# Window attention and two feed-forward layers on one core: a key ring of three blocks, a value block loaded twice, and earlier weight loads

## The chip, the cores and the metric

The kernel runs on 1 core of a Trainium2 chip. The metric is the device time of one execution in microseconds (us). It stands at 888.23 us before, the median of 3 runs (887.37 to 889.02).

## What is computed

Windowed attention (4 batches, 8 heads, 576 positions, head size 64, a window of 64 positions), and behind it two dense layers with 2304 tokens, d_model 512 and d_ff 2048. The weights are float64 in memory and are split on the chip into a high and a low float32r part; q, k and v are float32.

```python
scores = scale * np.matmul(q, k.transpose(0, 1, 3, 2))
rel = pos[:, None] - pos[None, :]
mask = (rel >= 0) & (rel < window)
attn = softmax(where(mask, scores, -1e9))
x = matmul(attn, v)                      # to (2304, 512)
r = np.maximum(x @ w_in, 0.0);  x = (r * r) @ w_out          # first layer
h = x @ w_in2;  out = (np.maximum(h, 0.0) + np.log1p(np.exp(-np.abs(h)))) @ w_out2
```

## The kernel before, in words

The 2304 rows are 18 "pairs" p of two 64-row blocks (a pair is 128 rows of all 8 heads). One pair runs through these jobs, whose names the text uses:

- Lq, Lk, Lv: loads of 256 KB each, issued by SyncE (SP). A row of a head is 64 floats.
- TK, TQ: transposes on TensorE (PE, line 528). CK, CQ: their copies out of PSUM, by VectorE (DVE) or ScalarE (ACT); CK writes `kT`, CQ scales q.
- CW (line 532, DVE): moves the last key block of the pair before to the third block of `kT`, since a pair needs its own two key blocks and the one before. V (line 611, DVE): copies the first 64 value rows of pair p into the buffer of pair p-1, so that one buffer holds the two value blocks that go together.
- S: mask and score matmuls on PE (lines 549 and 556); M (line 572, DVE): row maximum; E (line 581, ACT): exponent; N (lines 590 to 593, DVE): normalisation; PT, CP: transpose of the probabilities and copy; PV (line 619, PE): times the values; XH (ACT, line 630) and XL (DVE, line 633): x split into two parts.

The first layer runs over token tiles 0 to 4 of 384, 384, 512, 512 and 512 rows; pairs 0 to 2 make tile 0, pairs 3 to 5 tile 1. For tiles 0 and 1 a chunk f (128 of the 2048 hidden columns) of tile t is L0_t_f (x times w_in: 12 matmuls, lines 709 to 712), then Re, Sq and the split Gh (ACT) and Gl (DVE, line 757), then K0_t_f (times w_out: 12 matmuls, line 736). Each chunk needs a piece of w_in (f, 0) and of w_out (f, 1). A piece is loaded (LW, 512 KB, lines 350 and 355), then A (ACT, line 374), B, C, D, E (DVE, lines 377 to 393), F (ACT, line 400), G (DVE, line 404): five DVE steps each. Pieces then go to memory and are read back for the later tiles and the second layer, which work in blocks of seven products (PA to PD, lines 908 to 911). RZ (line 445) and SS (line 457) are DVE work on pieces for those blocks.

The order of all of it is worked out at build time by `Plan.order`, a list scheduler with a cost for each job and due times made from the table `WANTED`; every engine then runs its list in order, so an instruction that waits holds all behind it on its engine. At the start PE first waits for q of pair 0, transposes it, and runs 8 matmuls on an identity (`warm`, line 1097) that do nothing but run; they wait in the plan for `begin`, the clearing of `kT` and of a buffer of zero values (lines 1089 to 1091).

Of the kernel before, what the change touches and what calls it, by code (L numbers as in the profile page):

```python
# [10 lines left out]
F32 = mybir.dt.float32  # L11
# [11 lines left out]
    R0=254.26, RS=-0.27, T0=91.05, STEP0=0.29, A1=56.67, STEP1=4.99, B0=68.41, STEPB=2.68,  # L23
    T1=106.21, T2=160.86, LAP=93.92, C0=174.36, C1=484.25, PAIRS=106.74, SPAN=32.29,
# [155 lines left out]
def window_attention_moe_moe2(  # L180
# [80 lines left out]
    masks = const.tile([P, 3, P], BF16, name="masks")  # L261
    kT = const.tile([P, HP, P + W], F32, name="kT")
# [3 lines left out]
    def sel(m, a, half, pattern, base, mult):  # L266
        s = masks[W * a:W * a + W, m, W * half:W * half + W]
        nc.gpsimd.affine_select(
            out=s, in_=s, pattern=[[pattern, W]], compare_op=ALU.is_ge,
            fill=MASKED, base=base, channel_multiplier=mult,  # L270
        )

    def make_masks():


        nc.gpsimd.memset(masks, 0.0)
        for m in range(3):
            for a in range(2):
                own, before = (0, 1) if a == 0 else (1, 0)
                sel(m, a, own, -1, 0, 1)  # L280
                if m == a + 1:
                    sel(m, a, before, 0, -1, 0)
                else:
                    sel(m, a, before, 1, -1, -1)
# [72 lines left out]
    def add_weights(ph, n, f, which, want):  # L357
# [48 lines left out]
        def store(j):  # L406
# [12 lines left out]
            take=[("c", None, 1, [raw])] if ph else [], lag=3.2 if ph else 2.2,  # L419
            close=[("pro", (f"w1_{f}", 512 * i)) for i in range(2)] if not ph and late else [],  # L420
# [74 lines left out]
    def add_pair(p, at, step, loads_after):  # L495
# [7 lines left out]
        mask = masks[:, (1 if p in FIRST else 2 if p in FIRST2 else 0), :].rearrange("p (o f) -> p o f", o=1)  # L503
        mask = mask.to_broadcast([P, HP, P])
# [5 lines left out]
        def load(src, name):  # L510
            def fn(j):
                t = place(j, name, [P, DM], F32).rearrange("p (h d) -> p h d", h=H)
                done = 0
                while done < P:
                    b, s = divmod(p * P + done, S)
                    n = min(P - done, S - s)
                    nc.sync.dma_start(  # L517
                        out=t[done:done + n], in_=src[b, :, s:s + n, :].rearrange("h p d -> p h d")
                    )
                    done += n  # L520
            return fn
# [22 lines left out]
        def score(j):  # L544
            sc = [place(j, f"sc{p}_{e}", [P, HP, P], F32) for e in range(2)]
            qt = heads(live[f"q{p}"])
            if early:
                for e in range(2):
                    nc.tensor.matmul(out=sc[e], lhsT=ident16, rhs=mask, start=True, stop=False)

            for c in range(HP):
                kc = kT[:, c, :].rearrange("p (w s) -> p w s", w=3)
                for a in range(2):
                    for e in range(2):
# [4 lines left out]
                            rhs=kc[r, 0:2, :] if a else kc[r, 0:3:2, :],  # L559
# [3 lines left out]
        def add_mask(e):  # L563
            def fn(j):
                nc.vector.tensor_tensor(out=pr(e), in0=live[f"sc{p}_{e}"], in1=mask, op=ALU.add)
            return fn
# [76 lines left out]
        before = (f"S{p - 1}",) if p else ()  # L643
        for src, name in ((k, f"k{p}"), (q, f"q{p}"), (v, f"v{p}")):
            add(f"L{name}", {"DMA": 1.1}, load(src, name), loads_after, take=piece(name), lag=2.4, choice=from_top)
# [652 lines left out]
```

## Time and profile before

| what | value |
|---|---|
| median of 3 runs | 888.23 us |
| the profiled execution, its own time | 887.61 us |
| its span, first to last instruction | 885.8 us |
| granted TensorE clock, mean | 0.996 |
| PE busy | 859.0 us (97%) |
| DVE busy | 740.3 us (84%) |
| ACT busy | 596.1 us (67%) |
| moved by DMA | 254.35 MB, 287 GB/s |

The span is the time between first and last instruction of the profiled execution; 1.8 us of its own time lie around it. "Busy" counts overlapping instructions of one engine once; an engine that is busy can still be working on something that could have been done earlier. Idle time of an engine matters only where it ends in something that the last instruction needs.

### The profile page before, as it was taken

The numbers are of one execution on the slowest core, as the hardware profiler recorded it, in microseconds if no ns is written. First come the engines' busy times: TensorE is split into PE (matmuls) and PEld (weight loads), VectorE is DVE, ScalarE is ACT, GpSimd is POOL, SyncE is SP. The second block draws the span as 40 slices with busy tenths as digits, with TensorE's granted clock in tenths as the row PEclk, the third lists the DMA queues.
The fourth block names the chain that finished last, engine by engine and source line by source line (L and its number), as shares of the span: only waits on it lengthen the run. The fifth ranks groups of instructions, "written<-read, shape, count | busy, mean of one in ns | idle before, by whom it ended". The sixth has DMA issues, their size and how long they took to land.

```text
span 885.8 us, 17060 instructions
## 1 busy us (share of the span) xinstructions
PE 859.0 (97%) x6220; PEld 779.9 (88%) x6220; DVE 740.3 (84%) x1404; ACT 596.1 (67%) x1266; POOL 3.6 (0%) x19
## 2 busy tenths in 40 slices
PE   6799999999999999999999998999999999999998
PEld 5689999999888898888899987889999999999997
DVE  4999999799999987699676998898789678766854
ACT  5877876558675777467446775786677767666774
POOL 1000000000000000000000000000000000000000
PEclk9999999999999999999999999999999999999999
DMA  9999877999999999999999999988736872788571
GB/s 196 349 315 353 286 285 239 318 260 284 290 353 372 308 322 331 342 337 305 345 348 371 381 333 357 345 302 313 257 126 219 290 248 66 270 274 280 200 245 71
DMA packets 169986, 254.35 MB, mean 287 GB/s; under 512 B 65584, under 2 KB 119856, under 8 KB 169904
## 3 DMA queue, kind: packets, MB, share of 16 engines
q1 hardware_dynamic: 169904, 253.27, 86.6%
q8 instruction: 49, 0.80, 0.4%
q14 instruction: 33, 0.27, 0.1%
HBM read 193.46 MB, written 59.77 MB: 286 GB/s over the span
## 4 chain that ended last, share of the span: by engine, by line
PE 78%; DMA 8%; DVE 7%; ACT 3%; SPq 2%; issue 1%; DVEq 0%; ACTq 0%
PE acc L736 38%; PE pa L908 5%; PE pa L911 5%; PE pa L909 5%; PE pb L908 4%; PE pb L911 4%; PE pb L909 4%; PE h L709 2%; DMA area<-in_moe_w_out_dram 2%; PE h L710 2%; PE h L712 2%; DMA ri<-di 2%; SPq L517 2%; PE po L619 1%; DMA ro<-do 1%
## 5 line engine op out<-in xcount | busy, mean ns | idle before, releaser
L736 PE MATMUL acc<-ro,gh 128*128 128x512 f32 x576 | 179.2, 392 | 0.0
L736 PE MATMUL acc<-gh,ro 128*128 128x512 f32 x384 | 120.0, 394 | 0.0
L736 PEld LDWEIGHTS acc<-ro,gh 128*128 128x128 f32 x576 | 103.4, 189 | 17.7
L736 PE MATMUL acc<-ro,gl 128*128 128x512 f32 x288 | 112.3, 390 | 0.3 <-DVE gl L757 0.3
L908 PE MATMUL pb<-xT,ri 128*128 128x256 f32 x336 | 89.2, 288 | 0.0
L909 PE MATMUL pb<-xT,ri 128*128 128x256 f32 x336 | 87.7, 283 | 0.0
L1011 DVE SCALAR_TENSOR_TENSOR e<-u,e 128x512 f32<-128x512 f32 (+1 forms) x80 | 50.7, 634 | 39.6 <-ACT u L1005 39.6
L736 PEld LDWEIGHTS acc<-gh,ro 128*128 128x128 f32 x384 | 69.0, 189 | 12.0 <-issue 0.2
L736 PE MATMUL acc<-gl,ro 128*128 128x512 f32 x192 | 75.1, 391 | 0.0
L911 PE MATMUL pb<-xT,ri 128*128 128x256 f32 x336 | 67.7, 283 | 0.2 <-DVE xT L881 0.2
L736 PE MATMUL acc<-gh,w 128*128 128x384 f32 x256 | 67.1, 342 | 0.0
L908 PEld LDWEIGHTS pb<-xT,ri 128*128 128x128 f32 x336 | 63.7, 190 | 3.7 <-issue 0.3
L909 PEld LDWEIGHTS pb<-xT,ri 128*128 128x128 f32 x336 | 64.1, 191 | 2.6
L754 ACT CAST gh<-l 128x512 fp32r<-128x512 f32 (+1 forms) x80 | 45.6, 570 | 29.9 <-DVE l L1015 26.5
L736 PEld LDWEIGHTS acc<-ro,gl 128*128 128x128 f32 x288 | 54.1, 188 | 12.9 <-DVE gl L757 1.2
L757 DVE TENSOR_TENSOR gl<-l,gh 128x512 fp32r<-128x512 f32 (+1 forms) x80 | 50.5, 631 | 3.7 <-ACT gh L754 2.7
L911 PEld LDWEIGHTS pb<-xT,ri 128*128 128x128 f32 x336 | 52.3, 192 | 0.4 <-DVE xT L881 0.4
L1015 DVE TENSOR_TENSOR l<-l,e 128x512 f32<-128x512 f32 (+1 forms) x80 | 50.4, 631 | 1.5
L1003 ACT ACTIVATE e<-c 128x512 f32<-128x512 f32 (+1 forms) x49 | 27.0, 551 | 34.5 <-DVE c L951 12.2
L1006 ACT ACTIVATE l<-u 128x512 f32<-128x512 f32 (+1 forms) x80 | 47.2, 590 | 2.6
L1004 ACT ACTIVATE e<-e 128x512 f32<-128x512 f32 (+1 forms) x80 | 47.2, 590 | 2.5
L1005 ACT ACTIVATE u<-e 128x512 f32<-128x512 f32 (+1 forms) x80 | 47.2, 589 | 2.6
(231 smaller groups left out, 2298.3 us busy)
## 6 DMA issues: line engine op xcount, KB each, us to landing
ri<-di SPq DMA_DIRECT2D x154, 512.0 KB, 5.9
ro<-do SPq DMA_DIRECT2D x92, 512.0 KB, 5.8
ri<-di SPq DMA_DIRECT2D x46, 256.0 KB, 5.2
raw<-in_moe_w_in_dram SPq DMA_DIRECT2D x16, 512.0 KB, 8.9
raw<-in_moe_w_out_dram SPq DMA_DIRECT2D x16, 512.0 KB, 6.2
di<-w SPq DMA_DIRECT2D x32, 256.0 KB, 5.1
do<-w SPq DMA_DIRECT2D x16, 512.0 KB, 4.5
di<-osa SPq DMA_DIRECT2D x32, 256.0 KB, 6.0
```

The lines of the kernel that those rows point to most:

```text
L736: nc.tensor.matmul(o, lh, rh, start=st and i == 0, stop=sp and i == 2)
L754: nc.scalar.copy(out=place(j, f"gh{me}", [P, T], F32R), in_=live[src])
L757: nc.vector.tensor_tensor(out=place(j, f"gl{me}", [P, T], F32R), in0=live[src], in1=f32(live[f"gh{me}"]), op=ALU.subtract)
L908: nc.tensor.matmul(out, w[:, 0, c, :], x[:, 0, c, :], start=(c == 0), stop=False)
L909: nc.tensor.matmul(out, w[:, 1, c, :], x[:, 0, c, :], start=False, stop=False)
L911: nc.tensor.matmul(out, w[:, 0, c, :], x[:, 1, c, :], start=False, stop=(c == 1))
L1003: nc.scalar.activation(out=e, in_=live[src], func=AF.Abs)
L1004: nc.scalar.activation(out=e, in_=e, func=AF.Exp, scale=-1.0)
L1005: nc.scalar.add(u, e, 1.0)
L1006: nc.scalar.activation(out=g, in_=u, func=AF.Ln)
L1011: nc.vector.scalar_tensor_tensor(out=e, in0=u, scalar=1.0, in1=e, op0=ALU.subtract, op1=ALU.subtract)
L1015: nc.vector.tensor_tensor(out=live[f"l{me}"], in0=live[f"l{me}"], in1=live[f"e{me}"], op=ALU.add)
```

## The change

1. `kT` becomes a ring of three 64-column blocks: pair p writes its two blocks where p % 3 says, and scores read the right two of three; CW is gone. For p % 3 = 1 the two key blocks are loaded in reverse order, as two DMAs of 64 rows. The masks become seven 64-column kinds instead of three full ones (14 selections on GpSimd where there were 12), and pairs take two of them by a slice.
2. The value blocks of a pair are loaded twice, into `v` and a further buffer `u` (256 KB more for each of the 18 pairs); V is gone, and so is the clearing of a zero value buffer. `u` is one more buffer that a pair holds until PV.
3. The loads of k of pairs 0 to 2 are issued by ACT instead of SP.
4. `warm` waits for the identity alone and has the lowest rank, so it is first on PE.
5. Loads of weight pieces of the first layer get due times of their own (`W0`, `WS`), which puts them among the loads of the first pairs; the rest of `WANTED` has new numbers.

```diff
+    W0=-2.81, WS=5.37, R0=272.55, RS=-2.06, T0=90.01, STEP0=2.32, A1=50.92, STEP1=7.65, B0=50.27,
+    STEPB=3.01, T1=107.67, T2=159.56, LAP=88.87, C0=174.71, C1=472.98, PAIRS=115.66, SPAN=29.08,
...
-    masks = const.tile([P, 3, P], BF16, name="masks")
-    kT = const.tile([P, HP, P + W], F32, name="kT")
+    masks = const.tile([P, 7, W], BF16, name="masks")
+    kT = const.tile([P, HP, 3 * W], F32, name="kT")
...
             f"LW{me}", {"DMA": 1.45}, load, ["SS0_7" if ph else f"K0_0_{f - AHEAD}" if late else None],
+            rank=None if ph else WANTED["W0"] + WANTED["WS"] * ORDER.index((f, which)),
...
+        lie = {(0, 0): slice(0, 3, 2), (0, 1): slice(0, 2), (1, 0): slice(1, 3), (1, 1): slice(0, 3, 2),
+               (2, 0): slice(0, 2), (2, 1): slice(1, 3)}
...
-        def shift_k(j):
-            nc.vector.tensor_copy(out=kT[:, :, P:P + W], in_=kT[:, :, W:P])
-
         def copy_k(j):
-            copy(j.who, kT[:, :, 0:P], live[f"tk{p}"])
+            kb = kT.rearrange("p c (w s) -> p c w s", w=3)
+            copy(j.who, kb[:, :, lie[turned, 1], :], by_block(live[f"tk{p}"]))
...
-                            rhs=kc[r, 0:2, :] if a else kc[r, 0:3:2, :],
+                            rhs=kc[r, lie[turned, a], :],
...
-        def shift_v(j):
-            nc.vector.tensor_copy(out=live[f"v{p - 1}"][0:W], in_=live[f"v{p}"][0:W])
-
         def values(j):
-            vw = [live[f"v{i}"].rearrange("p (h d) -> p h d", h=H) for i in (p - 1, p)]
+            vw = [live[i].rearrange("p (h d) -> p h d", h=H) for i in (f"u{p}", f"v{p}")]
...
+        keys = pair[::-1] if turned == 1 else pair
+        around = [2 * p, max(2 * p - 1, 0)] if turned == 0 else [2 * p - 1, 2 * p]
+        for src, name, blocks in ((k, f"k{p}", keys), (q, f"q{p}", pair), (v, f"v{p}", keys), (v, f"u{p}", around)):
+            soon = p < 3 and src is k
...
-    add("begin", {"DVE": 2.0}, begin, ["ident"], 0.0, [("pro", None, 1, ["v-1"])], choice=from_top)
-    add("warm", {"PE": 2.5}, warm, ["begin"], 0.0, [("ps", "att0", 1, ["busy"])], ["busy"])
+    add("begin", {"DVE": 1.2}, begin, ["ident"], 0.0)
+    add("warm", {"PE": 2.5}, warm, ["ident"], -1.0, [("ps", "att0", 1, ["busy"])], ["busy"])
```

What that does to the order, at three places. First, the start of SP's list of loads, before (`prow` buffers hold q, k and v of the first pairs, `raw` a weight piece):

```order
L517 DMA prow_15_121<-in_q_dram 128x8x64
L517 DMA prow_15_121<-in_k_dram 128x8x64
L517 DMA prow_14_122<-in_q_dram 128x8x64
L517 DMA prow_13_123<-in_k_dram 128x8x64
L517 DMA prow_13_123<-in_q_dram 128x8x64
L517 DMA prow_12_124<-in_k_dram 128x8x64
L517 DMA prow_12_124<-in_v_dram 128x8x64
```

and of the change, SP first and then ACT, which issues the keys:

```order
L528 DMA prow_15_121<-in_q_dram 128x8x64
L344 DMA raw_0_0_141<-in_moe_w_in_dram 128x4x256
L528 DMA prow_13_123<-in_q_dram 128x8x64 x2
L344 DMA raw_1_0_205<-in_moe_w_in_dram 128x4x256
L528 DMA prow_12_124<-in_v_dram 64x8x64 x2
L528 DMA prow_12_124<-in_v_dram 128x8x64
L349 DMA raw_0_1_267<-in_moe_w_out_dram 128x1024
```

```order
L1273 ACT_TABLE_LOAD
L528 DMA prow_15_121<-in_k_dram 128x8x64
L528 DMA prow_14_122<-in_k_dram 64x8x64 x2
L528 DMA prow_14_122<-in_k_dram 128x8x64
L368 ACTIVATE z_0_0_207<-raw_0_0_141 128x512
L309 COPY kT<-tk_209 128x4x128
```

Where the first weight piece was the 17th kind of load in SP's list, it is now the second; seven pieces are issued before the loads of pair 3, and those wait for buffers that pair 0 gives back with PV0. ACT begins with the keys, and the first weight piece (A) stands before the copy of the first keys.

Second, the start of PE, before and with the change (`tq` and `tk` are the transposes, `busy` the eight matmuls that only run, `sc` the scores):

```order
L528 MATMUL tq_182<-ident,prow_15_121 128x128 x4
L1097 MATMUL busy<-ident 128x128 x8
L528 MATMUL tk_200<-ident,prow_15_121 128x128 x4
L528 MATMUL tq_205<-ident,prow_14_122 128x128 x4
L528 MATMUL tk_211<-ident,prow_13_123 128x128 x4
L528 MATMUL tq_218<-ident,prow_13_123 128x128 x4
L549 LDWEIGHTS ident_73
L549 MATMUL sc_0_223<-masks,ident_73 128x512
```

```order
L1108 MATMUL busy<-ident 128x128 x8
L538 MATMUL tq_200<-ident,prow_15_121 128x128 x4
L538 MATMUL tk_209<-ident,prow_15_121 128x128 x4
L538 MATMUL tk_215<-ident,prow_14_122 128x128 x4
L538 MATMUL tk_222<-ident,prow_14_122 128x128 x4
L538 MATMUL tq_227<-ident,prow_13_123 128x128 x4
L557 LDWEIGHTS ident_73
L557 MATMUL sc_0_236<-masks,ident_73 128x512
```

`busy` moved ahead of the first transpose. Ahead of the first scores stand the keys of all three pairs 0 to 2, where before there were those of pairs 0 and 1 and the queries of pairs 0 to 2.

Third, the start of DVE, before and with the change (`z` and `w` belong to a weight piece, `nm` is the maximum):

```order
L1090 MEMSET kT 128x768
L1091 MEMSET prow_14_122 64x512
L532 COPY kT<-kT 128x4x64
L542 TENSOR_SCALAR prow_14_122<-tq_205 128x512
L611 COPY prow_14_122<-prow_12_124 64x512
L532 COPY kT<-kT 128x4x64
L572 TENSOR_REDUCE nm<-sc_0_223 128x4
```

```order
L1102 MEMSET kT 128x768
L550 TENSOR_SCALAR prow_15_121<-tq_200 128x512
L371 TENSOR_SCALAR z_0_0_207<-z_0_0_207 128x512
L375 TENSOR_SCALAR z_0_0_207<-z_0_0_207 128x512
L381 SCALAR_TENSOR_TENSOR z_0_0_207<-raw_0_0_141,z_0_0_207 128x512
L387 SCALAR_TENSOR_TENSOR z_0_0_207<-raw_0_0_141,z_0_0_207 128x512
L309 COPY kT<-tk_215 128x4x2x64
L582 TENSOR_REDUCE nm<-sc_0_236 128x4
```

The shifts are gone, and the DVE steps of the first weight piece stand ahead of the first maximum. Further on, PE's list has five L0_1 chunks ahead of K0_0_11 where it had seven.

## Rows read from the trace of the kernel before

**Rows 1.** Busy time by stretch; last three columns: granted clock, DMA share, GB/s.

```profile
core 0: us, PE busy (x) PEld busy (x) DVE busy (x) ACT busy (x) POOL busy (x), PEclk, DMA share, GB/s
5.00:10.00 5.00, 5.00 (x35) 4.79 (x34) 0.69 (x1) 1.28 (x3) 0.00 (x0) 1.00 1.35 218
30.00:40.00 10.00, 6.69 (x59) 5.68 (x59) 9.85 (x24) 7.82 (x33) 0.00 (x0) 0.83 1.07 376
60.00:80.00 20.00, 20.00 (x117) 20.00 (x117) 19.67 (x41) 14.48 (x28) 0.00 (x0) 1.00 1.07 366
200.00:300.00 100.00, 99.36 (x848) 89.62 (x846) 95.98 (x191) 70.37 (x170) 0.00 (x0) 1.00 1.00 323
400.00:500.00 100.00, 96.78 (x607) 87.10 (x607) 79.37 (x146) 56.27 (x98) 0.00 (x0) 1.00 0.99 351
500.00:600.00 100.00, 97.17 (x614) 87.28 (x613) 92.66 (x158) 75.07 (x130) 0.00 (x0) 1.00 0.95 340
```

**Rows 2.** The chain of waits, in order of time (start, us, what).

```profile
46.21 1.20 DVE z L393 x2
49.64 0.34 DVE z L377
57.44 2.73 PE acc L736 x11
...
116.50 2.08 PE acc L736 x12
```

**Rows 3.** Timeline of DVE: first x part, the step after chunk 11, one RZ.

```profile
27.73 0.69 DVE L633 TENSOR_TENSOR xl<-po,xh 128x512 fp32r<-128x512 f32 x1
28.33 0.42 DVE L381 TENSOR_SCALAR z<-z 128x512 uint32<-128x512 uint32 x1
115.03 0.75 DVE L377 TENSOR_SCALAR z<-z 128x512 f32<-128x512 f32 x2
132.93 1.28 DVE L445 TENSOR_TENSOR z<-w 128x512 f32<-128x512 f32 x2
```

**Rows 4.** Timeline: issue of loads on SP, and the first value copy on DVE.

```profile
0.73 0.44 SPq L517 DMA_DIRECT2D prow<-in_q_dram  x1
4.85 1.14 SPq L517 DMA_DIRECT2D prow<-in_k_dram  x1
11.16 0.42 DVE L611 COPY prow<-prow 64x512 f32<-64x512 f32 x1 [1.44 <-DMA prow<-in_v_dram]
```

**Rows 5.** Timeline of ACT and PE in the first 40 us.

```profile
0.73 1.28 ACT L1262 ACT_TABLE_LOAD   x1 [0.73 <-PEq L1282]
4.93 3.19 PE L1097 MATMUL busy<-ident 128*128 128x128 f32 x16
9.71 0.59 PE L549 MATMUL sc<-masks,ident 128*128 128x512 bf16 x2
12.42 0.37 ACT L581 ACTIVATE prow<-sc,nm 128x128 f32<-128x128 f32 x1
15.08 0.24 ACT L581 ACTIVATION_READ_ACCUMULATOR prow<-sc,nm 128x1 f32 x1
19.55 1.10 PE L556 MATMUL sc<-kT,prow 64*64 64x128 f32 x32
33.90 0.63 PE L600 MATMUL pp<-ident,prow 128*128 128x128 f32 x4 [3.31 <-ACT prow L581]
34.89 1.99 PE L556 MATMUL sc<-kT,q 64*64 64x128 f32 x32
```

**Rows 6.** Groups by line, 0 to 160 us: the two shifts (DVE), a copy (ACT).

```profile
L532 DVE COPY kT<-kT 128x256 f32<-128x256 f32 x9 | 2.6, 284 | 0.0
L611 DVE COPY prow<-prow 64x512 f32<-64x512 f32 x4 | 1.6, 411 | 1.4 <-DMA prow<-in_v_dram 1.4
L315 ACT COPY kT<-tk 128x512 f32<-128x512 f32 x6 | 3.6, 601 | 4.2 <-PE tk L528 2.8 <-DVE kT L532 1.4
```

**Rows 7.** Who waited for whom: the longest of SP in the whole span.

```profile
SPq L1029 <- PE pa L911: 100.4, 55, 13.0
```

More of the change, by code (lines that the diff above doesn't have):

```diff
@@ L502, in add_pair, with by_block, load @@
         early = p < EARLY
-        mask = masks[:, (1 if p in FIRST else 2 if p in FIRST2 else 0), :].rearrange("p (o f) -> p o f", o=1)
-        mask = mask.to_broadcast([P, HP, P])
+        turned = p % 3
+        assert p not in FIRST or turned == 0
+        assert p not in FIRST2 or turned == 1
+        which = (slice(0, 4, 3) if p in FIRST else slice(0, 2), slice(1, 5, 3) if p in FIRST2 else slice(1, 3), slice(5, 7))
+        mask = masks[:, which[turned], :].rearrange("p (o w) s -> p o w s", o=1).to_broadcast([P, HP, 2, W])
+        lie = {(0, 0): slice(0, 3, 2), (0, 1): slice(0, 2), (1, 0): slice(1, 3), (1, 1): slice(0, 3, 2),
+               (2, 0): slice(0, 2), (2, 1): slice(1, 3)}
+        def by_block(t):
+            return t.rearrange("p h (w s) -> p h w s", w=2)
         def pr(e):
             return heads(live[f"{'kq'[e]}{p}"])
-        def load(src, name):
+        def load(src, name, blocks):
             def fn(j):
                 t = place(j, name, [P, DM], F32).rearrange("p (h d) -> p h d", h=H)
[L513 to L518, printed above, removed]
+                e = nc.scalar if j.who == "ACT" else nc.sync
+                runs = []
+                for i, n in enumerate(blocks):
+                    if runs and n == runs[-1][1] + runs[-1][2] and n * W % S:
+                        runs[-1][2] += 1
+                    else:
+                        runs.append([i, n, 1])
+                for i, n, m in runs:
+                    b, r = divmod(n * W, S)
+                    e.dma_start(
+                        out=t[i * W:(i + m) * W], in_=src[b, :, r:r + m * W, :].rearrange("h p d -> p h d")
                     )
-                    done += n
             return fn
@@ L641, in bank @@
             return [("ps", att, n, list(names))]
-        before = (f"S{p - 1}",) if p else ()
-        for src, name in ((k, f"k{p}"), (q, f"q{p}"), (v, f"v{p}")):
-            add(f"L{name}", {"DMA": 1.1}, load(src, name), loads_after, take=piece(name), lag=2.4, choice=from_top)
-        add(f"TK{p}", {"PE": 0.44}, turn("k"), [f"Lk{p}", f"S{p - 1}" if p > 3 else "begin"], at, bank(f"tk{p}"), lag=0.25)
-        add(f"CW{p}", {"DVE": 0.27}, shift_k, (*before, f"CK{p - 1}" if p else "begin"))
-        add(f"CK{p}", {"DVE": 0.61, "ACT": 0.52}, copy_k, [f"TK{p}", f"CW{p}"], give=[f"tk{p}"])
-        add(f"TQ{p}", {"PE": 0.44}, turn("q"), [f"Lq{p}", "begin"], at + 0.01, bank(f"tq{p}"), lag=0.25)
+        pair = [2 * p, 2 * p + 1]
+        keys = pair[::-1] if turned == 1 else pair
+        around = [2 * p, max(2 * p - 1, 0)] if turned == 0 else [2 * p - 1, 2 * p]
+        for src, name, blocks in ((k, f"k{p}", keys), (q, f"q{p}", pair), (v, f"v{p}", keys), (v, f"u{p}", around)):
+            soon = p < 3 and src is k
+            add(
+                f"L{name}", {"ACT": 0.9} if soon else {"DMA": 1.1}, load(src, name, blocks), loads_after, take=piece(name),
+                lag=2.8 if soon else 2.4, choice=from_top,
+            )
+        add(f"TK{p}", {"PE": 0.44}, turn("k"), [f"Lk{p}", f"S{p - 1}" if p > 3 else "warm"], at, bank(f"tk{p}"), lag=0.25)
+        add(
+            f"CK{p}", {"DVE": 0.61, "ACT": 0.52}, copy_k, [f"TK{p}", f"S{p - 1}" if p else "begin"], give=[f"tk{p}"]
+        )
+        add(f"TQ{p}", {"PE": 0.44}, turn("q"), [f"Lq{p}", "warm"], at + 0.01, bank(f"tq{p}"), lag=0.25)
         add(f"CQ{p}", {"ACT": 0.54, "DVE": 0.61}, copy_q, [f"TQ{p}"], give=[f"tq{p}"])
@@ L670, in add_pair @@
             )
[L671 removed]
         add(
[L673 to L674 removed]
+            f"PV{p}", {"PE": 1.15}, values, [f"CP{p}_0", f"CP{p}_1", f"Lv{p}", f"Lu{p}"], at + step * 5, bank(f"po{p}"),
+            [f"k{p}", f"q{p}", f"v{p}", f"u{p}"], lag=0.25,
         )
@@ L1090, in begin @@
         nc.vector.memset(kT, 0.0)
-        nc.vector.memset(place(j, "v-1", [P, DM], F32)[W:P], 0.0)
     def warm(j):
```

35 lines of the change are left out of this document (14 added, 21 removed).

## Prediction

> **What bounds the kernel now.** I read the busy time by stretch first [rows 1]. From 60 us on PE is full, with 20.00 of 20 us in the first such stretch, so what follows is paid by PE's own work, and a gain has to come from the time that PE lost before it. PE idles again only in the middle: 0.6 us between 200 and 300, 3.2 between 400 and 500, 2.8 between 500 and 600. The same rows show that DVE is busy for 19.67 of those 20 us as well: it splits the weight pieces that the chunks of tiles 0 and 1 consume, and in 30 to 40 us, where PE has only 6.69 of 10, DVE has 9.85. The chain of waits says the same: up to the first K chunk at 57.44 us it is made of loads and then of DVE steps; behind it stand whole K chunks of 2.08 us [rows 2]. So before 57 us the clock of the kernel is DVE, and it is slow to begin: at 5 to 10 us it is busy for 0.69 of 5 [rows 1].
>
> Why DVE begins late shows in the loads. Between 5 and 10 us the queues move 218 GB/s at a share of 1.35, against 376 GB/s in 30 to 40 us, where weights move [rows 1]. The first load's issue takes 0.44 us, a later one of the same size 1.14 [rows 4]: SP is held back by full queues, so these loads go at the pace of the DMA engines, 262 KB in 1.2 us.
>
> **The change part by part.** The sum goes to one point, chunk K0_0_11. I counted DVE's list up to each chunk in both orders and PE's chunks ahead of it; K0_0_11 has the least room in the new order. K0_0_9, counted the same way, allows 2.4 us, and the others more.
>
> *When the first scores run.* The first values of pair 0 were the seventh load, and DVE waited for them until 11.16 us [rows 4]: 7 x 0.262 MB at 218 GB/s is 8.4 us, so data flow from 2.7 us on. With the change, six loads of q and k and one weight piece (0.524 MB) lie ahead of the last key that S0 waits behind: 2.7 + 6 x 0.262 / 0.218 (7.2) + 0.524 / 0.376 (1.4) = 11.3 us. Two transposes (one like them is 0.63 us of busy time [rows 5], somewhat less where they overlap) and S0 starts at some 12.15 us, where it started at 9.71 [rows 5]. That part loses 2.4 us. Issuing keys from ACT costs nothing, since ACT waits for data anyway; its table load ends at 2.01 us [rows 5], so k of pair 0 is issued over a microsecond later than when it followed q on SP. That warm runs first costs nothing: its 3.19 us [rows 5] lie in the wait for q. The masks need two selections more on GpSimd, which is idle otherwise, and are done before S0.
>
> *From there to the first x part (XL0).* E0_0 started 2.7 us after S0 (12.42 after 9.71), so now at 14.85 us. From here ACT's list holds: six E, two CP, two A and XH0 up to XL0. Two E took 12.42 to 15.32 us [rows 5], so 1.45 each: 8.7 us; the five others take 0.60 [rows 6]: 3.0. XH0 ends at 26.55, XL0 takes 0.60 as the steps of that size do (1.20 for two) [rows 2], and ends at 27.15 us. Before, DVE went on from XL0 at 28.33 [rows 3]. The gain is 1.2 us: the first three pairs now run without the loads of pair 3 and 4 between them, and that outweighs the late start.
>
> *From XL0 to what K0_0_11 needs.* Before: 28.33 to 115.03 us [rows 3], 86.7 us. The new list has fewer steps in this stretch: the five of weight piece (0,0), now done while DVE waits for S0 (three of 0.60, two of 0.34 [rows 2]: 2.5 us); two key shifts and three value shifts (0.284 and 0.411 busy [rows 6], some 0.07 less as steps, as 0.60 is to 0.68: 1.4 us); one CK and two CP that went to ACT against one CQ that came (1.2 us less). It has one step more, RZ0_0 at 1.2 us, which stood at 132.93 before [rows 3]. Net 3.9 us less, 82.8 us. The inputs of K0_0_11 are complete at 27.15 + 82.8 = 109.95 us, and it starts at 110.1.
>
> *What PE has done by then.* Before, K0_0_11 started at 116.50 us [rows 2] with seven L0_1 chunks done; now five are, so 4.16 us of work lie behind it instead of ahead. The same progress was reached at 112.3 us before. Gain 112.3 - 110.1 = 2.2 us.
>
> *The rest.* Later shifts (12 of each kind from pair 6 on) run where PE is full or nearly so, and give nothing; if PE's waits in the middle came from DVE, at most the 6.7 us of idle time named above. The 18 further value loads are 4.7 MB. Three lie in the first 25 us, behind what S0 needs and ahead of PV0; twelve lie in the middle, where the DMA share is 1.00 [rows 1]. But SP's longest wait there is for PE to give ring buffers back, 100.4 us in 55 waits [rows 7], so the queues have room: nothing, with an upper bound in the rivals. The new numbers move jobs of the later tiles by a place or two; bounds are the 6.7 us of idle time gone, or as much added; I take nothing, since PE is 97 to 100% busy under either.
>
> Sum against the profiled execution: 887.61 - 2.2 = 885.4 us. The median of the runs lies 0.6 above that execution, so the forecast is **886.0 us**, 2.2 below 888.23. A measurement of this kernel can tell some 0.2% (1.8 us) from no change.
>
> **The rivals.** *The keys do not come in time (slower).* Keys and weights now stand in two queues of the same engines. If these took packets of both in turn, 256 bytes of a key against 1 KB of a weight, the 0.79 MB of three keys would pass 3.1 MB of SP's loads: 2.7 + 0.79 / 0.218 + 3.1 / 0.376 = 14.5 us instead of 11.3. S0 and XL0 come 3.2 us later, and the total is 889.2; anything later on, such as the copy of the fourth pair's q that DVE's list holds, adds to it, up to 890.5. It turns into a loss once the keys land after 13.5 us. For it: all of S0 waits behind the keys of three pairs. Against: before, 218 GB/s were kept with loads of one size.
>
> *A queue of its own helps (faster).* If issue on SP was the limit, ACT's queue adds to it, the keys land some 3 us sooner, and the time is 883.0. The issue of 0.44 us on an empty queue [rows 4] speaks against it. The Trainium skill, DMA: Bandwidth & Descriptors, section "Issuing engines are not separate DMA queues", says that loads started by several engines run on the same 16 DMA engines and only save issuing time; by that rule this rival falls, and the sum stays.
>
> *The clock falls (no change).* After 3.31 us of waiting PE's scores took 1.99 us instead of 1.10 [rows 5], with 0.83 granted over 30 to 40 us [rows 1]; 1.2 GHz is the lower level. With warm first and then waits of up to 2 us for each key, S0 and S1 may run at that level, 0.9 us longer each, of which some 1.3 reach XL0: 887.3. [...]
>
> *The middle gives it back (no change).* The twelve later value loads are 3.1 MB, 14.4 us of all queues at 218 GB/s. If a sixth of it came out as waits of PE for ring buffers, 2.4 us: 888.4.
>
> **How the numbers follow.** Forecast 0.45, late keys 0.20, own queue 0.12, clock 0.10, middle 0.13. The forecast's own spread is some 1 us, so most of it is faster by over 0.2% (below 886.5). Faster: 0.36 of the forecast and 0.12, together 0.48. Within: 0.08 of the forecast, the clock, 0.08 of the middle, 0.05 of late keys, together 0.31. Slower: 0.01, 0.05 and 0.15, together 0.21. The range goes from 882.5 (own queue, or half of the middle's idle time gone) to 890.5 (late keys with what follows).
>
> **What would show it.** Right: first scores at about 12 us, XL0 ending near 27, K0_0_11 (the twelfth K chunk) near 110 with PE full behind it, no line for shifts, PE idle in 200 to 600 us as before. Wrong: scores after 13.5 us or before 10; granted clock below 1.00 before 20 us; PE idle between 60 and 110 us; longer waits of PE for ring buffers.

## The result, and the profile after

The changed kernel takes **897.15 us** (median of 17 runs, 894.03 to 901.97), the kernel before in the same comparison 888.66 (17 runs, 886.06 to 894.71): ratio **1.0094, 95% interval 1.0078 to 1.0110**, some 8.4 us slower. The forecast was 886.0 us, its range ended at 890.5. The profiled execution has a span of 894.5 us (885.8 before), PE busy for 864.3 us, DVE for 731.9 (740.3 before: the shifts are gone), and 259.07 MB moved.

Busy time by stretch in the changed kernel, columns as in [rows 1]:

```profile
10.00:15.00 5.00, 4.65 (x48) 3.30 (x48) 1.02 (x3) 1.88 (x4) 0.00 (x0) 0.70 1.09 298
25.00:30.00 5.00, 5.00 (x71) 4.22 (x69) 3.71 (x9) 2.37 (x7) 0.00 (x0) 0.50 0.30 68
200.00:300.00 100.00, 96.32 (x832) 87.14 (x832) 84.33 (x165) 66.83 (x162) 0.00 (x0) 1.00 0.99 313
300.00:400.00 100.00, 95.76 (x800) 83.87 (x798) 82.24 (x160) 62.21 (x154) 0.00 (x0) 1.00 1.00 321
400.00:500.00 100.00, 97.30 (x603) 86.67 (x604) 78.04 (x143) 56.73 (x98) 0.00 (x0) 1.00 0.97 343
500.00:600.00 100.00, 96.69 (x605) 85.77 (x605) 93.56 (x163) 71.68 (x122) 0.00 (x0) 1.00 0.96 345
```

The first, second and fourth of these stretches in the kernel before:

```profile
10.00:15.00 5.00, 3.57 (x73) 2.45 (x72) 2.80 (x8) 3.63 (x17) 0.00 (x0) 1.00 1.35 217
25.00:30.00 5.00, 4.90 (x107) 4.02 (x108) 4.77 (x12) 4.45 (x11) 0.00 (x0) 1.00 1.07 337
300.00:400.00 100.00, 99.00 (x826) 87.77 (x825) 84.68 (x169) 66.19 (x160) 0.00 (x0) 1.00 1.01 326
```

Two things differ. The granted clock now falls within the first 30 us, to its lower level of 1.2 GHz (0.50) from 25 to 30 us; in the kernel before it fell only after that, to 0.83 over 30 to 40 us [rows 1]. And PE, idle for 0.64 us between 200 and 300 and for 1.00 between 300 and 400 before, is idle for 3.68 and 4.24. From 400 us on PE's idle time is nearly as before. What PE waits for in 200 to 420 us (us in total, times, longest):

```profile
PE tk L538 <- DMA k<-in_k_dram: 3.4, 2, 1.7
PE po L624 <- DMA v<-in_v_dram: 1.7, 2, 1.3
PE acc L748 <- ACT gh L766: 1.6, 1, 1.6
```

All that the kernel before has there:

```profile
PE pa L908 <- ACT wk L315: 3.0, 2, 2.0
PE po L619 <- DVE q L315: 0.6, 1, 0.6
```

So that stretch had no wait of PE for a load. The first of the new ones is for k13, the keys of pair 13. SP issues it at 247.70 us, and PE stands at its transposes (timeline of SP and PE, columns start, us, what, and the idle time just before):

```profile
247.70 1.29 SPq L528 DMA_DIRECT2D k<-in_k_dram  x2
255.44 0.63 PE L538 MATMUL tk<-ident,k 128*128 128x128 f32 x4 [1.73 <-DMA k<-in_k_dram]
```

The same two rows of the kernel before: the load goes out 9.7 us ahead of its use (7.7 in the changed kernel), and nothing waits.

```profile
231.75 1.35 SPq L517 DMA_DIRECT2D k<-in_k_dram  x2
241.44 0.60 PE L528 MATMUL tk<-ident,k 128*128 128x128 f32 x4
```

The start came nearly as forecast. The warm-up, the second and the last key, the mask of pair 0, the first PV and the first XL in the timeline of the changed kernel:

```profile
1.36 3.78 PE L1108 MATMUL busy<-ident 128*128 128x128 f32 x16 [1.36 <-POOL ident masks.py:199]
9.12 0.67 PE L538 MATMUL tk<-ident,prow 128*128 128x128 f32 x4 [2.55 <-DMA prow<-in_k_dram]
10.35 1.11 PE L538 MATMUL tk<-ident,prow 128*128 128x128 f32 x4 [0.55 <-DMA prow<-in_k_dram]
12.11 1.04 PE L557 MATMUL sc<-masks,ident 128*128 128x512 bf16 x2
25.36 1.98 PE L624 MATMUL po<-prow,prow 128*64 128x64 f32 x32
28.03 0.69 DVE L638 TENSOR_TENSOR xl<-po,xh 128x512 fp32r<-128x512 f32 x1 [0.60 <-ACT xh L635]
```

K0_0_11 in its chain of waits:

```profile
111.82 2.37 PE acc L748 x12
```

S0 begins at 12.11 us (forecast 12.15), but the mask takes 1.04 us where it took 0.59 [rows 5] and PV 1.98, so XL0 ends near 28.7 instead of 27.15 and K0_0_11 starts 1.7 us later than forecast. Against 112.3 us, the same progress before, that leaves 0.5 us of the 2.2. Between the end of the warm-up at 5.14 us and S0, PE had nothing but transposes and, between them, two longer waits of 2.55 and 0.55 us; there the clock fell.

Where the rest went: between K0_0_15 and PA0_3_0 (135.41 to 391.48 us before, 133.10 to 397.50 after) PE's list holds 249.2 us of work before and 251.3 after (one L0_1 chunk more), each job at its undisturbed duration. PE lost 6.8 us there before and 13.1 after, and its idle time in that stretch rose from 1.6 to 7.7 us, 5.1 of them at the loads of k and v above. This is the "loss of the middle" in the expectations below. From PA0_3_0 to the end the changed kernel takes another 2.7 us more (497.0 for 494.3). PE is idle there as long as before (10.0 us for 9.9), so these 2.7 us are not such waits; what they are stays open.

### The profile page after: what moved, and what is told of

It is laid out like the page before. It is cut to its first block, busy times and chain, and to the rows that moved or that the text cites. A ratio compares the mean times of both kernels' runs of the same rounds, so it can differ in the third digit from the quotient of the medians.

```text
span 894.5 us, 17055 instructions
## 1 busy us (share of the span) xinstructions
PE 864.3 (97%) x6220; PEld 779.8 (87%) x6220; DVE 731.9 (82%) x1368; ACT 596.6 (67%) x1265; POOL 4.4 (0%) x21
## 2 busy tenths in 40 slices
DMA packets 188930, 259.07 MB, mean 290 GB/s; under 512 B 84528, under 2 KB 138800, under 8 KB 188848
## 4 chain that ended last, share of the span: by engine, by line
PE 63%; DVE 14%; DMA 12%; SPq 4%; ACT 3%; issue 2%; DVEq 0%; ACTq 0%
PE acc L748 32%; PE pa L920 4%; PE pa L923 4%; PE pa L921 4%; DMA ri<-di 3%; PE pb L920 3%; PE pb L923 3%; PE pb L921 3%; DMA area<-in_moe_w_out_dram 2%; SPq L528 2%; PE h L721 2%; PE h L722 2%; PE h L724 2%; PE po L624 1%; DVE gl L769 1%
## 5 line engine op out<-in xcount | busy, mean ns | idle before, releaser
L309 ACT COPY wk<-pa 128x512 f32<-128x512 f32 x56 | 32.4, 581 | 26.9 <-PE pa L923 26.6
```

The source lines that it names most:

```text
L309: (nc.scalar.copy if e == "ACT" else nc.vector.tensor_copy)(out=out, in_=in_)
```

## The experiments

Every run stands beside runs of the kernel before on the same chip, which took 889.7 to 890.8 us there; so I compare ratios to it, and turn them into us at 888.7 (the changed kernel: +8.4 us). The theory was that the middle loses time to loads that the planner (the list scheduler) sends too late; the rivals were the bytes of u and the new numbers of the order.

**e6: the clock at the start.** The changed kernel with fillers where PE waits.

```diff
+                for _ in range({"k1": 8, "k2": 2}.get(f"{what}{p}", 0)):
+                    nc.tensor.matmul(out=pk[:, 0, :], lhsT=ident, rhs=ident, start=True, stop=True)
...
+                for _ in range((2 if not p and not e else 4) if p < 2 else 0):
+                    nc.tensor.matmul(out=pp[:, 0, :], lhsT=ident, rhs=ident, start=True, stop=True)
```

> The changed kernel with 24 more matmuls of the kind that warms the engine, put where PE waits in the first 25 us: 8 ahead of the transposes of k1, 2 ahead of those of k2, and 14 ahead of the transposes of the probabilities of pairs 0 and 1; they write a tile that the transposes write over. Theory of the start: the granted clock, 0.70 in 10 to 15 us and 0.50 in 25 to 30 us, cost 1.5 us of the 2.2 us that the earlier first stage should give. With the fillers the clock is 0.95 or more in both stretches, the mask of pair 0 takes 0.6 us (1.04 in the changed kernel), the first PV 1.2 us (1.98), and K0_0_11 starts near 110.3 (111.8); the time falls by about 1.5 us, to 895.7. Rival: the start is set by ACT and DVE alone; the clock rises and K0_0_11 starts at 111.5 or later, the time within 0.5 us of the changed kernel. The loss in the middle stays in both.

Measured: 896.31 us, ratio 1.0061 (1.0038 to 1.0083), +5.4 us. A stretch of e6, then its timeline, then its chain of waits:

```profile
25.00:30.00 5.00, 4.58 (x85) 3.84 (x80) 4.93 (x12) 3.27 (x7) 0.00 (x0) 1.00 0.77 193
```

```profile
11.63 0.59 PE L559 MATMUL sc<-masks,ident 128*128 128x512 bf16 x2
23.98 1.15 PE L628 MATMUL po<-prow,prow 128*64 128x64 f32 x32
```

```profile
109.60 0.18 PE acc L752
```

The clock is back at 1.00, mask and PV have their old durations, and K0_0_11 starts at 109.60, 2.2 us before the changed kernel and slightly before the forecast's 110.1. So the clock took the gain of the start; whether it fell for the waits or because only transposes ran between them, e6 doesn't part, since its fillers change both. In the profile the 2.2 us are lost again by 360 us, since PE then stands at the same late loads, for 2.46 us at k16; the medians are 2.9 us apart, with intervals that touch. What the whole time gains stays open.

**e7, e2: the twelve later loads of u, without them and with long packets.** e7 leaves the loads out, and PV reads v in their place; e2 keeps their bytes but takes them from rows of 2 KB instead of 256 bytes, so from other places in v.

In e7:

```diff
+                if name[0] == "u" and p >= 6:
+                    return
...
-            vw = [live[i].rearrange("p (h d) -> p h d", h=H) for i in (f"u{p}", f"v{p}")]
+            vw = [live[i].rearrange("p (h d) -> p h d", h=H) for i in (f"u{p}" if p < 6 else f"v{p}", f"v{p}")]
```

In e2:

```diff
+                if name[0] == "u" and p >= 6:
+                    e.dma_start(out=t.rearrange("p h d -> p (h d)"), in_=src.rearrange("b h s d -> (b h s d)")[0:P * DM].rearrange("(p f) -> p f", p=P))
+                    return
```

> The changed kernel, in its own order, without the twelve loads of u from pair 6 on; PV of these pairs reads v in place of u, so half of its sums are over other values. PE's work stays. It parts the bytes from the rest: in e2, where the twelve loads kept their bytes and lost seven eighths of their packets, the loss between K0_0_15 and PA0_3_0 fell from 6.2 us (changed kernel against the kernel before) to 3.8. Rival 'bytes': the transfers of the middle are the bound, 3.1 MB less at some 315 GB/s are 10 us of the DMA engines, so all of the loss goes and more: 889 to 891 us. Theory 'just in time': k13 and k16 are issued as late as before, PE still waits 2 us or more for k and v between 250 and 370 us: 893 to 895.

> The changed kernel, in its own order of instructions, with each of the twelve loads of u from pair 6 on as one DMA of the same bytes whose rows are 2 KB long in DRAM, in place of rows of 256 bytes. It reads other values than the ones wanted, so the attention of pairs 6 to 17 is computed from other data. Theory 'just in time': the late loads are those of k, v and q of pairs 13 and 16, whose place in the order stays; a gain of under 2 us (895 to 897). Rival 'bytes' in its form 'small packets': the twelve loads cost the queue their packets; with an eighth of the packets the loads behind them land 1 to 3 us earlier, PE's waits for k and v go, and the time falls to 890 to 893.

Measured: e7 892.08 us, ratio 1.0035 (1.0017 to 1.0053), 5.2 us less than the changed kernel in the same order; e2 896.44 us, 1.0065 (1.0039 to 1.0091), whose interval reaches the changed kernel's. In e7 PE still waits for k and v between 200 and 420 us, but less (3.4 and 1.7 above):

```profile
PE tk L540 <- DMA k<-in_k_dram: 2.0, 2, 1.7
PE po L626 <- DMA v<-in_v_dram: 0.4, 1, 0.4
```

The loads of u cost 5.2 us. e7 came out between its two forecasts: both "bytes" and what stays of "just in time" are real. e2 lies where "just in time" put it, but whether packets or bytes weigh more it doesn't settle.

**e12: the bytes alone, in the order of the kernel before.**

```diff
+    twice = [dpool.tile([P, DM], F32, tag=f"tw{i}", name=f"tw{i}") for i in range(18)]
...
+                    if name[0] == "v" and p >= 6:
+                        spare = twice[p].rearrange("p (h d) -> p h d", h=H)
+                        nc.sync.dma_start(
+                            out=spare[done:done + n], in_=src[b, :, s:s + n, :].rearrange("h p d -> p h d")
+                        )
```

> The kernel before in its own order on every engine, with twelve more transfers in SP's queue: behind the load of v of each pair from 6 on, the same rows once more (256 KB, rows of 256 bytes), from DRAM to a spare place in DRAM that nobody reads. Nothing waits for them. Theory 'full DMA engines': from 200 to 600 us the DMA share is 0.95 to 1.00, so what is added there pushes the loads behind it back and PE waits; e7 gave 4.4 us back in the middle when these bytes went, so 892 to 894 us here. Rival 'order': it is not the bytes but the redrawn order of the pairs, the weights and the chunks that costs; with the order of the kernel before kept, the time stays within 889 to 890.5.

Measured: 904.14 us, ratio 1.0154 (1.0122 to 1.0187), **+13.7 us**. Its added transfers between 200 and 400 us (median us to landing), and a stretch of it:

```profile
tw<-in_v_dram SPq DMA_DIRECT2D x6, 256.0 KB, 5.8
```

```profile
300.00:400.00 100.00, 94.42 (x785) 83.54 (x785) 78.27 (x156) 61.73 (x151) 0.00 (x0) 0.97 0.99 312
```

PE's longest wait between 200 and 420 us, and the chain of waits that leads to it:

```profile
PE pa L914 <- ACT wk L316: 4.5, 1, 4.5
```

```profile
331.52 9.84 DMA area<-in_moe_w_out_dram
342.03 0.58 ACT wk L316
```

Nobody waits for these transfers, and apart from their issues on SP no engine's order is another. PE is idle for 5.6 us of that stretch, for 1.0 before. Its longest wait goes through ACT to a weight piece that took 9.84 us to land; the medians between 200 and 400 us rose from 6.8 to 8.1 us for such pieces of w_out and from 6.7 to 7.8 for the 512 KB loads of `ri` (pieces read back, the largest group), while those of w_in stayed (6.1 for 6.4). So added transfers hold up the loads behind them while the DMA share is near 1.00, and that is paid. The time was forecast at 894 us at most; the price came out well above that, and above that of u; each transfer is also written to DRAM, which may be why. Two things are not parted: SP also spends time on issuing them, and 2.2 us of the profile's loss stand ahead of K0_0_11 (PE starts it at 118.5 us for 116.3), most of it before the first of them is issued at 57.5 us. In e9 below, with nothing added, K0_0_11 is as late.

**e1, e3, e14: the order in the changed kernel.** e1 gives the planner a longer time to landing (which redraws PE's list as well), e3 the six old middle numbers, e14 is e7 with e3's numbers.

In e1:

```diff
-                lag=2.8 if soon else 2.4, choice=from_top,
+                lag=2.8 if soon else 2.4 if p < 6 else 8.0, choice=from_top,
```

In e3 and e14:

```diff
-    STEPB=3.01, T1=107.67, T2=159.56, LAP=88.87, C0=174.71, C1=472.98, PAIRS=115.66, SPAN=29.08,
+    STEPB=3.01, T1=107.67, T2=160.86, LAP=93.92, C0=174.36, C1=484.25, PAIRS=106.74, SPAN=32.29,
```

> The changed kernel, with the planner told that a load of a pair from 6 on takes 8.0 us behind its issue to land, where it was told 2.4. The loads of pairs 12 to 17 then go out earlier (k13, for one, 13 places earlier in SP's order of 568). Theory 'just in time': in the middle PE waits for loads of pairs that the planner sends out too late (TK13, PV13, TK16, PV16). Then PE's waits for k and v loads between 250 and 370 us (4 to 6 us in the profile of the changed kernel) fall under 1 us, and the kernel takes about 891 to 893 us, against 897.2 of the changed one. Rival 'bytes': the 12 more value loads fill the DMA engines in the middle, whatever the order; the waits move to other transfers and the time stays within 895 to 899. Rival 'numbers': the loss lies in the place of the pairs between the chunks (the numbers of the order), so this stays at 895 to 899 too.

> The changed kernel, with six numbers of the order back to those of the kernel before (T2, LAP, C0, C1, PAIRS, SPAN: where the later pairs, the weights of the second expert and the chunks of the middle are wanted); the first stage keeps the new numbers. Rival 'numbers': the loss of 7 us between 250 and 370 us goes, and the kernel takes 889 to 891 us. Theory 'just in time': the planner's price of a load is the same, pairs are again issued late by it, only at other places; the waits of PE for loads stay at 3 us or more in all and the time at 894 to 898. Rival 'bytes': as the theory, 895 to 898.

> The changed kernel with both suspects taken out: no loads of u from pair 6 on (as e7, where PV of these pairs reads v in place of u, other values) and the six middle numbers of the kernel before (as e3). Theory 'bytes and numbers': e7 took some 5 us from the time and e3 some 3; together 8, so 888.5 to 890.5 us, the time of the kernel before. Rival 'only one of them counts': either alone clears the way and the other adds nothing, 891 to 893 us. Rival 'a third thing' (the first stage itself, as e8 hints, which had neither and took 898.9): 895 or more.

Measured: e1 894.95 us, ratio 1.0059 (1.0037 to 1.0081); e3 894.65, 1.0050 (1.0032 to 1.0068), 3.9 us less than the changed kernel; **e14 889.06, 0.9989 (0.9970 to 1.0008)**, the time of the kernel before. Waits of PE in 200 to 420 us, e3 first, then all that e14 has:

```profile
PE pp L610 <- DVE sm L600: 2.0, 1, 2.0
...
PE po L624 <- DMA v<-in_v_dram: 0.7, 2, 0.4
PE tq L538 <- DMA q<-in_q_dram: 0.3, 1, 0.3
```

```profile
PE pp L612 <- DVE sm L602: 1.4, 1, 1.4
PE acc L750 <- DVE gl L771: 0.4, 1, 0.4
```

```profile
300.00:400.00 100.00, 100.00 (x843) 89.88 (x842) 87.94 (x171) 68.49 (x164) 0.00 (x0) 1.00 0.98 332
```

With the old numbers the waits for loads fall from 5.1 us to 1.0; without u they are gone, and PE is full from 300 to 400 us (the last line, of e14). u (5.2) and the middle numbers (3.9) add up to nearly the 9.3 us that e14 is below the changed kernel; by the intervals, each of these differences is known to some 2 us. e1 took away the waits for k and v, as the first theory has it, yet a wait of 2.4 us of PV for ACT stands in their place: late issue is how part of the loss shows, not all of it. In time e1 and e3 come out near the lower end of the cases that expected the loss to stay (894 or 895 us and up), and e14 where its first case put it.

**e9, e10, e4: the numbers in the kernel before.** Its code, with the middle numbers (e9), the first-stage numbers (e10), both (e4).

In e9:

```diff
-    T1=106.21, T2=160.86, LAP=93.92, C0=174.36, C1=484.25, PAIRS=106.74, SPAN=32.29,
+    T1=106.21, T2=159.56, LAP=88.87, C0=174.71, C1=472.98, PAIRS=115.66, SPAN=29.08,
```

In e10:

```diff
-    R0=254.26, RS=-0.27, T0=91.05, STEP0=0.29, A1=56.67, STEP1=4.99, B0=68.41, STEPB=2.68,
-    T1=106.21, T2=160.86, LAP=93.92, C0=174.36, C1=484.25, PAIRS=106.74, SPAN=32.29,
+    R0=272.55, RS=-2.06, T0=90.01, STEP0=2.32, A1=50.92, STEP1=7.65, B0=50.27, STEPB=3.01,
+    T1=107.67, T2=160.86, LAP=93.92, C0=174.36, C1=484.25, PAIRS=106.74, SPAN=32.29,
```

> The kernel before with the six middle numbers of the changed kernel alone (T2, LAP, C0, C1, PAIRS, SPAN); the first stage keeps its own. e4 with all new numbers took 898.0 us. Theory 'redrawn order': all of it comes in the middle, 895 to 899 us. Rival: e4 lost its time at the start (K0_0_11 4 us later for the same work), and this takes 890 to 893 us.

> The kernel before with the first-stage numbers of the changed kernel alone (R0, RS, T0, STEP0, A1, STEP1, B0, STEPB, T1); the middle keeps its own. e9, with the middle numbers alone, took 901.2 us, e4, with both, 898.0. Theory: the middle numbers carry the loss, and this takes 888 to 892 us. Rival: either set by itself breaks the fit of the two, 896 or more.

> The kernel before, its code untouched, with the new numbers of the order that it knows (all but the two for the first weights). Theory: the numbers alone cost the middle 1 to 2 us, as e3 showed the other way round; the start changes by under 2 us either way; 888 to 892 us. Rival 'numbers': most of the 8.5 us are theirs, 894 to 898 us.

Measured: e9 901.17 us, ratio 1.0126 (1.0095 to 1.0157); e10 895.27, 1.0066 (1.0042 to 1.0090); e4 897.98, 1.0101 (1.0071 to 1.0132). My expectation for e4 missed by 6 us, and the rival beside it holds. Numbers alone cost the kernel before 11.2, 5.9 and together 9.0 us: they don't add. In e9 PE's longest waits between 200 and 420 us are for ACT's work on the pairs (the exponent, a copy), not for loads; that these pairs stand too close to their chunks is likely, but not shown:

```profile
PE pp L600 <- ACT q L581: 2.9, 1, 2.9
PE pp L600 <- ACT k L315: 2.5, 1, 2.5
```

**e11, e13: does any redrawing of the order cost?** Half a microsecond on one number of the kernel before (e11 C0=174.86, e13 LAP=94.42).

In e13:

```diff
-    T1=106.21, T2=160.86, LAP=93.92, C0=174.36, C1=484.25, PAIRS=106.74, SPAN=32.29,
+    T1=106.21, T2=160.86, LAP=94.42, C0=174.36, C1=484.25, PAIRS=106.74, SPAN=32.29,
```

> The kernel before with one number of the order changed by half a microsecond (C0 174.86 for 174.36), which redraws the order a little: the first difference on PE is its 208th job of 541, and 18 places of PE and 35 of SP differ. No work, byte or wait is added. Theory 'redrawn order': what the numbers of the kernel before have is a fit to the chip that any redrawing loses, in part even here; 890 to 893 us. Rival: such a change does nothing, 888 to 890 us.

> The kernel before with LAP 94.42 for 93.92, half a microsecond again, which redraws far more: 122 of PE's 541 places and 105 of SP's 553 differ. No work, byte or wait is added. Theory 'redrawn order': 893 to 898 us, as far from the kernel before as the other numbers in e4 (898.0). Rival: the later numbers of the changed kernel are bad for a reason of their own (the pairs later, the lap shorter), and half a microsecond does nothing: 888 to 891 us.

Measured: e11 888.74 us, ratio 0.9988 (0.9971 to 1.0005); e13 887.46, **0.9973 (0.9957 to 0.9989)**. The theory of the redrawn order falls: 122 moved places of PE cost nothing, and e13 beats both kernels by a little. That an order is new costs nothing by itself in these two cases; it is the values of the new numbers that cost. Which of them, and through which job, no run shows.

**e5, e8, e15: other mixtures.** e5 is the changed code with all old numbers and no rank for the first weights. e8 keeps ring and u for pairs 0 to 5 and shifts on DVE from pair 6 on, with e3's numbers and e6's fillers; e15 is e8 without the fillers.

The core of e8 and e15 (RING is 6):

```diff
-    masks = const.tile([P, 7, W], BF16, name="masks")
+    masks = const.tile([P, 8, W], BF16, name="masks")
...
+        ring = p < RING
+        turned = p % 3 if ring else 0
...
+        if p > RING:
+            add(f"CW{p}", {"DVE": 0.27}, shift_k, [f"S{p - 1}", f"CK{p - 1}"])
...
+        if not ring:
+            add(f"V{p}", {"DVE": 0.35}, shift_v, [f"Lv{p}", f"PV{p - 1}"])
```

> The changed code (ring, values twice, warm first, keys of the first pairs by ACT) with all the numbers of the order of the kernel before and no rank of their own for the first weights. Theory (twelve loads in a full middle): the later loads cost what they cost in the changed kernel, less the 1.4 us that e3 took from the middle; the start gains nothing without the weights at the front, so 893 to 896 us. Rival 'numbers': without the new numbers the structure costs nothing in the middle, 888 to 891 us.

> A version meant to beat both: the changed kernel up to pair 5 (ring, values twice, weights early) with the 24 warming matmuls of e6, and from pair 6 on the keys and values of the kernel before (a 0.27 us shift of keys and a 0.35 us shift of values on DVE for each pair, no load of u), with the six middle numbers of e3. Theory (the clock in the start, twelve loads in the middle): K0_0_15 starts near 131 us (135.4 before, less 2.2 us of PE work that is done later), the loss between K0_0_15 and PA0_3_0 is 6.8 us as in the kernel before, and the time is 2 us under the kernel before: 886 to 887. Rival 'absorbed': e6 gained 2.2 us at the start and lost them by PA0_3_3, since the middle is set by its transfers and not by PE; then this takes 888 to 890.

> e8 without its 24 warming matmuls: ring, values twice and early weights up to pair 5, from pair 6 on the shifts of the kernel before, and the old middle numbers. It differs from e14 in the middle by the shifts of keys and values on DVE (0.62 us for each of twelve pairs) and by reading the right values. Theory 'the shifts take DVE's time': 893 to 897 us, above e14 by 4 or more. Rival 'the fillers': PE's work ahead of the first PV held the first stage back in e8, and without them this takes 888 to 891 us, as e14.

Measured: e5 898.68 us, ratio 1.0115 (1.0091 to 1.0140); e8 898.92, 1.0115 (1.0085 to 1.0144); e15 902.06, 1.0117 (1.0081 to 1.0153). All three are slower than every case named for them. e5 shows that the new first-stage numbers belong to the new structure: with them and the early weights, e3 is at 1.0050. e8 and e15 have one thing in common that I had not meant to change: an eighth mask.

**e18, e17, e19: 128 bytes of address.** A tile that nobody touches, between kT and area: 128 bytes per partition in the changed kernel (e18), 256 in e15 (e17), 128 in the kernel before (e19).

In e18 and e19:

```diff
+    const.tile([P, 32], F32, name="spare")
     area = const.tile([P, 8 * 384], F32, name="area")
```

> The changed kernel in its own order, with a spare tile of 128 bytes per partition, that nobody touches, between kT and area, which puts every tile behind it where e15 has it (256 bytes above a multiple of 512). Theory 'address': the first 20 us move 225 GB/s (263 in the changed kernel), S0 starts near 14 us (12.1), and the time rises by 5 us or more, to 902 or above. Rival: nothing changes, 896 to 898 us, and e15 is slow for its order.

> e15 in its own order, with a spare tile of 256 bytes per partition, that nobody touches, between kT and area, so that every tile behind it starts at a multiple of 512 bytes again, as in the kernel before (in e15, whose masks have eight parts, at 256 above one; in the changed kernel, whose masks have seven, at 128 above one). Theory 'address': in the profiles of e8 and e15 the first 20 us moved 222 and 224 GB/s where the changed kernel moved 263 with the same transfers, and S0 was 2 us later; the address of the tiles makes the transfers slower all through the full middle. Then the first 20 us move 255 or more, S0 starts near 12.1 us and the time falls to 886 to 891 us. Rival 'order': addresses do nothing, S0 stays near 13.9 and the time at 899 to 903.

> The kernel before in its own order, with a spare tile of 128 bytes per partition, that nobody touches, between kT and area, so that every tile behind it starts where the changed kernel has it (128 bytes above a multiple of 512). e18 moved the changed kernel's tiles by the same 128 bytes, and it took 901.8 us for 897.2, with 222 GB/s in the first 20 us for 263. Theory 'address' (where these tiles lie sets the rate of the transfers into them, and the place that the changed kernel has is the faster one): 220 GB/s or more in the first 20 us (193 in the kernel before), S0 near 9 us or earlier (9.71), and 883 to 886 us. Rival: the place matters only with the changed kernel's first transfers (two queues); S0 and the time stay, 888 to 891 us.

Measured: e18 901.76 us, ratio 1.0129 (1.0111 to 1.0146), against 1.0094 (1.0078 to 1.0110) without the spare tile, intervals that just miss each other; e17 899.14, 1.0107 (1.0080 to 1.0133), as e15; e19 888.31, **0.9973 (0.9955 to 0.9992)**, less of a gain than the 883 to 886 us expected. The first 20 us of the changed kernel and its loads of k in them (size, median us to landing):

```profile
0.00:20.00 20.00, 13.94 (x146) 11.01 (x146) 9.58 (x19) 9.06 (x32) 4.39 (x21) 0.91 1.02 263
```

```profile
prow<-in_k_dram ACTq DMA_DIRECT2D x2, 256.0 KB, 5.9
```

The same of e18:

```profile
0.00:20.00 20.00, 13.80 (x110) 10.80 (x110) 6.87 (x13) 6.26 (x16) 4.39 (x21) 0.83 1.11 222
```

```profile
prow<-in_k_dram ACTq DMA_DIRECT2D x2, 256.0 KB, 7.1
```

The same of the kernel before:

```profile
0.00:20.00 20.00, 12.57 (x142) 10.39 (x146) 9.33 (x22) 10.38 (x39) 3.63 (x19) 1.00 1.11 193
```

```profile
prow<-in_k_dram SPq DMA_DIRECT2D x4, 256.0 KB, 4.9
```

And of e19:

```profile
0.00:20.00 20.00, 14.14 (x166) 11.49 (x166) 10.18 (x24) 10.49 (x40) 3.65 (x19) 1.00 0.91 207
```

```profile
prow<-in_k_dram SPq DMA_DIRECT2D x4, 256.0 KB, 4.4
```

The same loads in the same order land 0.5 to 1.2 us sooner or later by where their tiles lie. All profiles say the same: 4.9 to 5.0 us in all seven of the kernel before and its variants without the spare tile; 5.6 to 6.2 in seven with the changed start at the place of the changed kernel, 7.0 to 7.4 in the four at other places (e8, e15, e17, e18). The price comes at the start: K0_0_11 starts 4.0 us later in e18 than in the changed kernel. Seven masks of 128 bytes stand where three of 256 stood, so the change moved every later tile by 128 bytes, and that was a gain. At e18's place the changed kernel is 11.5 us slower than the kernel before, so the rest of the change costs more than its own time shows. For e17, which I took to be at a good place, the theory as I had put it fails: e18 and e17 lie 256 and 512 bytes behind the kernel before, both at the slow rate (222 and 224 GB/s for 263). In the four places tried (0, 128, 256 and 512 bytes) what counts is the 128 bytes within 256. If e15 pays some 3 us for its place, as e18 does, it is still 8 us behind e14; that stays open (its order differs, and DVE has the shifts).

## Why the prediction was wrong

For the fourth point below, the wait of SP that [rows 7] gives for the whole span, in the kernel before between 200 and 420 us alone:

```profile
SPq L1029 <- PE pa L911: 17.1, 8, 3.6
```

- *When the first scores run*: right in the number, S0 at 12.11 us for 12.15, but by luck, since two errors cancelled: the last key was there at 10.35 us for 11.3, as the tiles had moved (in e18 its transposes begin at 12.26), and the steps behind it took longer at the low clock. ACT's queue brought little: with the tiles at the same place, e5, whose first keys go out by ACT, moved 214 GB/s in the first 10 us, and e19, with all loads on SP, 192. That is 0.2 MB more, some 1 us of loads, and not the 3 us of the rival "a queue of its own helps", which is out. The Trainium skill, DMA: Bandwidth & Descriptors, section "Issuing engines are not separate DMA queues", says that loads started by several engines share the same 16 DMA engines, and that only issuing time is saved; these two runs agree.
- *From there to the first x part*: the term lacked the clock, which stood among the rivals at a chance of 0.10 and a price of 1.3 us. It cost 2.2 us at K0_0_11 (111.82 against 109.60 in e6), as much as the whole forecast gain.
- *From XL0 to what K0_0_11 needs* and *What PE has done by then*: with the clock at 1.00 the point came at 109.60 us for 110.1. The count of DVE's steps held: from XL0's end at 28.72 us, 82.8 us more give 111.5, and K0_0_11 started at 111.82.
- *The rest*, the twelve loads of u: **this step failed**. It took them as "nothing", because SP waits longest for ring buffers [rows 7], "so the queues have room". The row was misread: it counts the whole span, and in the kernel before only the 17.1 us above of it stand between 200 and 420 us. In the changed kernel the whole wait is 102.1 us in 56 waits, as long as before, and yet the loads cost time. SP's wait for a buffer doesn't mean that the DMA engines are idle: they worked at a share of 1.00 between 200 and 300 us in the kernel before [rows 1]. e7 gives these loads 5.2 us, and e12 shows with PE's order kept that added transfers delay others that PE needs. The rival "the middle gives it back" had the place, but 2.4 us for the price, and the wrong wait: the late loads are k and v, and PE stands at them, not at ring buffers.
- *The rest*, the new numbers: **failed too**. "I take nothing" with bounds of 6.7 us either way; the middle numbers cost 3.9 us in the changed kernel, and 11.2 in the kernel before. PE's 97% busy was no argument: 3% of 886 us are 27 us. What in the new values costs this stays open. (The 6.7 us leave out the 1.0 us of idle time between 300 and 400.)
- *The rest*, the later shifts that "give nothing": not tested. e15, which has them, is far behind e14, which doesn't, but differs in order and place too.
- The range ended at 890.5 since the one slow case was about the start. No case let the middle cost more than 2.4 us, though the bounds named beside it allowed it. With u and the new middle numbers both out (e14), the kernel is where the kernel before is, at 0.9989.
- Not seen at all: the masks' size moves all later tiles.

## What to carry to other kernels

Where the DMA share is near 1.00, price every added transfer in full, at the rate of that stretch, until an experiment shows it hidden (3.1 MB at 313 GB/s would be 10 us; 5.2 were measured for u and 13.7 for e12's copies, so this is an estimate and not a bound); a queue that waits for buffers is no proof of room. Test the parts of a change apart: here a start that brought 0.5 us of 2.2, loads that cost 5.2, numbers that cost 3.9 and a lucky shift of 128 bytes stood under one time. In this kernel's start, warming matmuls paid between the waits too, and not only at the front, at least up to K0_0_11.

## What the runs showed of the hardware that was not expected

A shift of 128 bytes per partition in the place of SBUF tiles changes how fast rows of 256 bytes land in them: 0.5 us of 4.9 in the kernel before (e19), 1.2 of 5.9 in the changed one (e18), 0.27% and 0.35% of the whole time. The place is counted from the first tile in the code; the absolute address isn't shown by any run. The Trainium skill, DMA: Bandwidth & Descriptors, section "How a descriptor splits into AXI transactions", says that a transaction must start at a multiple of 256 bytes, and that a descriptor which doesn't begins with one from the multiple below. By an estimate from this, a row of 256 bytes that lies 128 off would take two transactions instead of one. That would fit, if the first tile itself lies 128 bytes off such a multiple, which no run here shows.
